# Loads of q, k and v moved to other slots of the pair loop, v split one slot earlier

## The chip, the cores and the metric

The kernel runs on one core of a Trainium2 chip. The metric is the time of one execution on the device, in microseconds. A core has five engines with queues of their own: TensorE (PE in the profile; its weight loads are PEld), VectorE (DVE), ScalarE (ACT), GpSimd (POOL) and SyncE (SP), which in this kernel issues all DMAs. Each engine works through its queue in order, and an instruction waits at the head of its queue until what it depends on is done.

## The reference

Sigmoid attention over 8 batches of 12 heads, 448 positions of 64 numbers, then a bilinear feed-forward network over all 3584 tokens:

```python
scores = scale * np.matmul(q, k.transpose(0, 1, 3, 2)) - np.log(S)
attn = 1.0 / (1.0 + np.exp(-scores))
x = np.matmul(attn, v)          # then heads side by side: 3584 x 768
a = x @ w1                      # 768 x 1024
b = x @ w2
h = a * b @ w3                  # 1024 x 1024
return h @ w_out                # 1024 x 768
```

The weights reach the kernel as 64-bit words, and are decoded to 32-bit numbers on the chip. Most products are made from a high and a low half of each operand, so that one product is three matmuls (hi x hi, hi x lo, lo x hi).

## The kernel before

The work is a loop over 48 **pairs** of heads (6 pairs to a batch, 8 batches), with four **slots** to a pair, one for each chunk of 128 keys (the last one has 64, and is taken second: `chunks` = 0, 3, 1, 2). Slot s belongs to pair s // 4. In a slot PE does the scores of its chunk (`scores` or, for the short chunk of a split pair, `short_scores`), then 12 matmuls of `up`, the feed-forward product of the batch before (`take(filler, ups)`, from slot 26 on; one output group `fc` takes three slots and ends with a store of `g`), then the product of the slot before with v (`attend_due`, tile `av`). `combine` makes x of a pair after its last attend: ScalarE and VectorE bring the two banks of `av` together in the tile `t`, and then split it into `xh`, `xl`.

Pairs 0 to 8 (`PLAIN` = 9) are **plain**: q and k are used as loaded, one tile `qp` for both. Pairs 9 to 47 are **split**: `split_pair` (lines 151 to 166) makes `qs` (two VectorE operations, lines 158 and 159), `kh` (VectorE, line 66), `kl` (POOL, line 67) and `ks` (four POOL copies, line 165), and needs the tiles `qq` and `kk`, one buffer each. `split_v` (168 to 176) makes `vs` by two VectorE casts and two POOL subtractions. All of `qp`, `qq` and `kk` share three buffers (tag `qk`); `vv` has two, the split tiles have two each.

`load_pair` (123 to 138) issues the loads of q and k, two DMAs for a plain pair and four for a split one; `load_v` (140 to 149) issues two or three. Before the change both are called at the start of a pair (lines 392 to 396): q and k for the pair after next, v for the next pair; v of the pair itself is split there too, and `split_pair` for the next pair is called in slot 1 (line 406).

Between these goes the decoding of the weights (`decode_weights`, 293 to 310), in 32 **jobs**: jobs 0 to 15 are w1 and w2, from 16 on w3. A job loads its words (`raw`, line 74), takes their magnitude on ScalarE (line 79), has six VectorE operations (lines 86 to 102), and is then split into halves (line 309, by lines 66 and 67). Jobs 0 to 11 have three buffers of words, loaded two jobs ahead; from job 12 on there is one buffer, and a job's words are loaded once the job before is decoded (line 303). Jobs 9 to 15 begin in slots 28, 29, 31, 32, 34, 35 and 38. Jobs 2 fc and 2 fc + 1 are first used by `up` in slot 26 + 3 fc of the passage.

The order of PE and SP is that of the program throughout (`manual_schedule`). That of ScalarE and POOL is, up to the start of pair 8; VectorE's order, and that of the other two from pair 8 on, is laid out by a planner ahead of the run, which goes by the place in the program and by when it thinks operands ready. Which of the free buffers of a tag a tile gets is also the planner's choice.

After the loop come the last batch's `up`, the product of w3 and w_out (line 484), and the final product with the stored `g` (line 500).

Of the kernel before, what the change touches and what calls it, by code (L numbers as in the profile page):

```python
# [25 lines left out]
def sigmoid_attention_bilinear_ffn(  # L26
# [22 lines left out]
    NC = len(CHUNKS)  # L49
# [6 lines left out]
    PLAIN = 9  # L56
# [8 lines left out]
    def split(dst_hi, dst_lo, src, hi_engine, lo_engine):  # L65
        hi_engine(out=dst_hi, in_=src)  # L66
        lo_engine.tensor_tensor(out=dst_lo, in0=src, in1=dst_hi, op=ALU.subtract)  # L67
# [55 lines left out]
    def load_pair(b, hp):  # L123
        heads = slice(2 * hp, 2 * hp + 2)
        if b * NPAIR + hp < PLAIN:

            qk = pa.tile([P, 2, S], F32, name="qp", tag="qk", bufs=3)
            for i, src in enumerate((qT, kT)):
                nc.sync.dma_start(out=qk[:, i], in_=src[b, heads].rearrange("h d s -> (h d) s"))
            return qk[:, 0], qk[:, 1]  # L130
        qq = pa.tile([P, 2, S], F32, name="qq", tag="qk", bufs=3)
        kk = pa.tile([P, 2, S], F32, name="kk", tag="qk", bufs=3)
        for dst, src in ((qq, qT), (kk, kT)):
            for r in range(2):
                nc.sync.dma_start(
                    out=dst[r * D:(r + 1) * D], in_=src[b, heads].rearrange("h d s -> d h s")
                )
        return qq, kk

    def load_v(b, hp):  # L140
        vv = pa.tile([P, NC, 2 * D], F32, name="vv")
        cols = slice(hp * 2 * D, (hp + 1) * 2 * D)
        full = (NC - 1) * P
        nc.sync.dma_start(
            out=vv[:, :NC - 1], in_=v[b, :full, cols].rearrange("(c p) e -> p c e", p=P)
        )
        for r in range(1 if b * NPAIR + hp < PLAIN else 2):
            nc.sync.dma_start(out=vv[r * D:(r + 1) * D, NC - 1], in_=v[b, full:, cols])
        return vv

    def split_pair(plain, qq, kk):

        if plain:
            return qq, kk, None, None
        qs = pf[0].tile([P, 2, S], F32R, name="qs")
        kh = pf[0].tile([P, 2, S], F32R, name="kh")
        kl = pf[0].tile([P, 2, S], F32R, name="kl")
        nc.vector.tensor_copy(out=qs, in_=qq)
        nc.vector.tensor_tensor(out=qs[D:], in0=qq[D:], in1=qs[D:], op=ALU.subtract)
        split(kh, kl, kk, nc.vector.tensor_copy, nc.gpsimd)  # L160

        ks = pf[0].tile([P, 2, P], F32R, name="ks")
        for j in range(2):
            for i, k in ((j, kh), (1 - j, kl)):
                nc.gpsimd.tensor_copy(out=ks[:, j, i * D:(i + 1) * D], in_=k[:, j, S - D:])
        return qs, kh, kl, ks

    def split_v(plain, vv):
        if plain:
            return vv  # L170

        vs = pf[0].tile([P, NC, 2, 2, D], F32R, name="vs")
        for j in range(2):
            split(vs[:, :, j, j, :], vs[:, :, j, 1 - j, :], vv[:, :, j * D:(j + 1) * D],
                  nc.vector.tensor_copy, nc.gpsimd)
        return vs
# [12 lines left out]
    def scores(qs, kh, kl, c):  # L189

        at, n = CHUNKS[c]
        sp = ps.tile([P, 2, 512], F32, name="sp", bufs=2)[:n, :, :S]
        for j in range(2):
            if kl is None:
                rows = slice(j * D, (j + 1) * D)
                nc.tensor.matmul(sp[:, j], kh[rows, at:at + n], qs[rows], start=True, stop=True)  # L196
                continue
            for m, k in enumerate((kh, kl)):
                nc.tensor.matmul(sp[:, j], k[:, j, at:at + n], qs[:, j], start=m == 0, stop=m == 1)  # L199
        return sp  # L200

    def attention(plain, sp):

        n = sp.shape[0]
        if plain:
            a = pa.tile([P, 2, S], F32, name="ap", tag="ah", bufs=3)[:n]
            sigmoid(a, sp)
            return (a,)
        ah = pa.tile([P, 2, S], F32R, name="ah", tag="ah", bufs=3)
        sigmoid(ah[:n], sp)  # L210
        sigmoid(sp, sp)
        if n < P:

            nc.vector.tensor_tensor(out=ah[n:], in0=sp, in1=ah[:n], op=ALU.subtract)
            return (ah,)
        al = pf[0].tile([P, 2, S], F32R, name="al")
        nc.vector.tensor_tensor(out=al, in0=sp, in1=ah, op=ALU.subtract)  # L217
        return ah, al

    def short_scores(ks, qs):  # L220


        sp = ps.tile([P, 2, 512], F32, name="sp", bufs=2)[:, :, :S]
        for j in range(2):
            nc.tensor.matmul(sp[:, j], ks[:, j], qs[:, j], start=True, stop=True)  # L225
        t = pf[0].tile([P, S], F32, name="st", bufs=1)
        add_halves(t, [sp[:, j] for j in range(2)])
        return t

    def short_attention(t):  # L230

        a = pa.tile([P, 2, S], F32R, name="ah", tag="ah", bufs=3)
        for j in range(2):
            rows = slice(j * D, (j + 1) * D)
            sigmoid(a[rows, j], t[rows])
        sigmoid(t, t)
        for j in range(2):
            rows, others = slice(j * D, (j + 1) * D), slice((1 - j) * D, (2 - j) * D)
            nc.vector.tensor_tensor(out=a[others, j], in0=t[rows], in1=a[rows, j], op=ALU.subtract)  # L239
        return (a,)  # L240
# [52 lines left out]
    def decode_weights():  # L293

        for i, (n, at, cs, _) in enumerate(jobs):
            if i + 2 < EARLY:
                load_job(i + 2)
            for k in (i, i + 1):
                if k not in fs and k in raws:
                    fs[k] = magnitude(raws[k])  # L300
            f = decode(raws.pop(i), fs.pop(i))
            if i + 1 >= EARLY and i + 1 < len(jobs):
                load_job(i + 1)
            if n == 3:
                nc.sync.dma_start(out=w3_dram[at, :, cs], in_=f)
                yield
                continue
            yield
            split(wh[n][:, at, cs], wl[n][:, at, cs], f, nc.scalar.copy, nc.vector)
            yield  # L310
# [24 lines left out]
    def take(stream, n):  # L335
        for _ in range(n):
            next(stream, None)
# [5 lines left out]
    pairs = [(b, hp) for b in range(B) for hp in range(NPAIR)]  # L343
# [8 lines left out]
    qks, vvs = {}, {}  # L352
    for p in range(2):
        qks[p] = load_pair(*pairs[p])
        load_job(p)
        if p == 0:
            vvs[0] = load_v(*pairs[0])
    splits, vs = {0: split_pair(0 < PLAIN, *qks.pop(0))}, {}
    weights = decode_weights()
    xs = {b: [] for b in range(B)}  # L360
    filler = iter(())
# [4 lines left out]
    def attend_due(slot):  # L366
        while waiting and waiting[0][0] <= slot:
# [6 lines left out]
            if c == NC - 2:  # L374
                b = pairs[p][0]
                xs[b].append(combine(b, accs.pop(p)))
                del vs[p]

    chunks = [0, NC - 1, *range(1, NC - 1)]
# [2 lines left out]
    for p, (b, hp) in enumerate(pairs):  # L384
        if p == PLAIN - 1:
            order.close()
            order.enter_context(tc.manual_schedule(engines={ET.PE, ET.SP}))
        plain = p < PLAIN
        if p == PLAIN - 1:
            phase_p.close()  # L390
            pf.append(phase_a.enter_context(tc.tile_pool(name="pf", bufs=2, side="right")))
        if p + 2 < len(pairs):
            qks[p + 2] = load_pair(*pairs[p + 2])
        if p + 1 < len(pairs):
            vvs[p + 1] = load_v(*pairs[p + 1])
        vs[p] = split_v(plain, vvs.pop(p))
        qs, kh, kl, ks = splits.pop(p)
        for i, c in enumerate(chunks):
            if not plain and i == 1:
                short = short_scores(ks, qs)  # L400
            else:
                sp = scores(qs, kh, kl, c)
                if not plain and i == 2:
                    waiting.append((slot + 1, p, NC - 1, short_attention(short)))
                waiting.append((slot + 1, p, c, attention(plain, sp)))
            if i == 1 and p + 1 < len(pairs):
                splits[p + 1] = split_pair(p + 1 < PLAIN, *qks.pop(p + 1))
            take(weights, steps.count(slot))
            if b > 0 and (hp, i) == (0, 2):
                take(filler, 10 ** 6)  # L410
                filler = up(b - 1, xs[b - 1], itertools.repeat("up"))
            take(filler, ups)
            attend_due(slot)
            slot += 1
# [124 lines left out]
```

## Time and profile before

| | |
|---|---|
| time, median of 3 runs | 1111.47 us (1111.01 to 1111.79) |
| the profiled execution | 1109.63 us, its span 1107.6 us |
| PE busy | 1070.8 us (97%), 5076 matmuls |
| DVE busy | 729.3 us (66%) |
| ACT busy | 563.0 us (51%) |
| POOL busy | 222.7 us (20%) |
| chain that ended last | PE 87%, DVE 6%, DMA 2%, ACT 2% |

Times in the rows are microseconds from the start of the span. A busy share is a mean over the whole span; matmuls are pipelined, so the duration of a single one (0.37 us) is longer than the distance from one to the next (0.2 us). An idle time in brackets stands before the instruction, with what ended it. A DMA row of SP is the issue, not the transfer.

### The profile page before, as it was taken

What the parts mean: (1) busy time and instruction counts of PE and PEld (TensorE: products, weight loads), DVE (VectorE), ACT (ScalarE), POOL (GpSimd) and SP (SyncE); (2) the same over time, 40 slices, a digit from 0 to 9 for tenths busy, and PEclk for the clock granted to TensorE, in tenths of its full rate; (3) what the DMA queues carried; (4) which work ended last, traced back from release to release, by engine and by line L of the source; (5) the groups of instructions that cost most, each with busy time, mean ns of one, the idle gap of its engine ahead of it and who ended that gap; (6) DMA issues with size and microseconds to landing.
All of it is one profiled execution on the core that took longest, in us unless ns stands there. A gap on an engine that the chain in (4) does not pass through costs nothing.

```text
span 1107.6 us, 14080 instructions
## 1 busy us (share of the span) xinstructions
PE 1070.8 (97%) x5076; PEld 910.5 (82%) x5076; DVE 729.3 (66%) x1073; ACT 563.0 (51%) x789; POOL 222.7 (20%) x277
## 2 busy tenths in 40 slices
PE   7996959999999999999999999999999999999998
PEld 1253749899899989989889999999999988888887
DVE  6876787788888878888797887857873132122221
ACT  5843647666776767767767776663342111011100
POOL 0001133243343333343333332400000000000000
PEclk9998979999999999999999999999999999999999
DMA  8634365444454434525454343206453021333211
GB/s 257 195 94 125 88 153 148 106 119 111 110 140 128 133 105 122 128 83 136 114 139 129 92 136 86 78 17 201 133 204 109 10 101 71 123 127 130 86 48 47
DMA packets 100692, 129.14 MB, mean 117 GB/s; under 512 B 8016, under 2 KB 82960, under 8 KB 100624
## 3 DMA queue, kind: packets, MB, share of 16 engines
q1 hardware_dynamic: 100624, 128.25, 39.7%
q8 instruction: 40, 0.66, 0.2%
q14 instruction: 28, 0.23, 0.1%
HBM read 98.34 MB, written 29.88 MB: 116 GB/s over the span
## 4 chain that ended last, share of the span: by engine, by line
PE 87%; DVE 6%; DMA 2%; ACT 2%; issue 1%; SPq 1%; POOL 0%; DVEq 0%; POOLq 0%; ACTq 0%
PE up L320 39%; PE up L500 21%; PE av L255 10%; PE sp L199 8%; PE up L484 6%; DMA raw<-w 2%; PE sp L225 1%; PE sp L196 1%; PE av L248 1%; DVE raw L99 1%; DVE f L94 1%; ACT f L79 1%; DVE raw L86 1%; DMA vv<-vL 1%; DVE al L217 1%
## 5 line engine op out<-in xcount | busy, mean ns | idle before, releaser
L320 PE MATMUL up<-xh,w 128*128 128x448 f32 x1536 | 468.2, 368 | 2.3 <-DVE g L331 2.3
L320 PEld LDWEIGHTS up<-xh,w 128*128 128x128 f32 x1536 | 288.9, 188 | 35.7 <-issue 5.3
L320 PE MATMUL up<-xl,w 128*128 128x448 f32 x768 | 281.6, 367 | 0.0
L500 PE MATMUL up<-w 128*128 128x512 f32 x1008 | 228.7, 389 | 0.0
L500 PEld LDWEIGHTS up<-w 128*128 128x128 f32 x1008 | 189.2, 188 | 39.3
L180 ACT ACTIVATE ah<-sp,bias 128x896 fp32r<-128x896 f32 x117 | 117.8, 1006 | 97.2 <-PE sp L199 97.1
L217 DVE TENSOR_TENSOR al<-sp,ah 128x896 fp32r<-128x896 f32 x117 | 127.5, 1090 | 44.2 <-ACT sp L180 42.5
L320 PEld LDWEIGHTS up<-xl,w 128*128 128x128 f32 x768 | 144.5, 188 | 12.9
L67 POOL TENSOR_TENSOR kl<-kk,kh 128x896 fp32r<-128x896 f32 x39 | 104.5, 2678 | 246.4 <-DVE kh L66 195.0
L510 DVE COPY o_sb<-up 128x512 f32<-128x512 f32 x42 | 29.0, 691 | 161.0 <-PE up L500 161.0
L66 ACT CAST w<-graw 128x1024 fp32r<-128x1024 f32 x28 | 29.3, 1055 | 174.7 <-PE up L500 170.5
L67 POOL TENSOR_TENSOR vs<-vv,vs 128x256 fp32r<-128x256 f32 x78 | 67.2, 874 | 251.8 <-DVE vs L66 182.7
L255 PE MATMUL av<-ah,vs 128*128 128x448 f32 x312 | 103.7, 373 | 13.9 <-POOL vs L67 12.7
L180 ACT ACTIVATE sp<-sp,bias 128x896 f32<-128x896 f32 x117 | 113.8, 973 | 0.0
L199 PE MATMUL sp<-qs,kh 128*128 128x448 f32 x234 | 86.3, 369 | 0.0
L199 PE MATMUL sp<-qs,kl 128*128 128x448 f32 x234 | 86.2, 368 | 0.0
L255 PE MATMUL av<-al,vs 128*128 128x448 f32 x234 | 86.2, 368 | 0.0
L239 DVE TENSOR_TENSOR ah<-st,ah 64x448 fp32r<-64x448 f32 x78 | 56.1, 719 | 40.0 <-ACT st L180 38.8
L255 PEld LDWEIGHTS av<-ah,vs 128*128 128x128 f32 x312 | 58.7, 188 | 25.4 <-POOL vs L67 13.7
L79 ACT ACTIVATE f<-raw 128x768 f32<-128x768 f32 (+2 forms) x48 | 34.1, 711 | 64.5 <-DMA raw<-w 28.2
L86 DVE TENSOR_SCALAR raw<-raw 128x768 uint32<-128x768 uint32 (+2 forms) x48 | 35.6, 743 | 38.1 <-ACT f L79 37.9
L186 ACT COPY t<-av 64x448 f32<-64x448 f32 x78 | 41.2, 529 | 34.0 <-PE av L255 33.0
(54 smaller groups left out, 1289.3 us busy)
## 6 DMA issues: line engine op xcount, KB each, us to landing
qq<-qT SPq DMA_DIRECT2D x78, 224.0 KB, 3.6
kk<-kT SPq DMA_DIRECT2D x78, 224.0 KB, 3.8
g_dram<-g SPq DMA_DIRECT2D x64, 224.0 KB, 1.9
graw<-g_dram SPq DMA_DIRECT2D x14, 1024.0 KB, 5.3
raw<-w SPq DMA_DIRECT2D x16, 768.0 KB, 6.2
out<-o_sb SPq DMA_DIRECT2D x42, 256.0 KB, 2.0
vv<-vL SPq DMA_DIRECT2D x48, 192.0 KB, 3.8
raw<-w3T SPq DMA_DIRECT2D x16, 512.0 KB, 4.9
```

The lines of the kernel that those rows point to most:

```text
L67: lo_engine.tensor_tensor(out=dst_lo, in0=src, in1=dst_hi, op=ALU.subtract)
L79: nc.scalar.activation(f, raw[..., 1].bitcast(F32), AF.Abs, scale=HW_SCALE)
L86: nc.vector.tensor_scalar(out=high, in0=high, scalar1=0x80000000, scalar2=0x80000000, op0=ALU.bitwise_and, op1=ALU.bitwise_xor,)
L180: nc.scalar.activation(dst, src, AF.Sigmoid, bias=bias[:n], scale=scale)
L186: nc.scalar.copy(out=dst[rows], in_=src[j][others])
L199: nc.tensor.matmul(sp[:, j], k[:, j, at:at + n], qs[:, j], start=m == 0, stop=m == 1)
L217: nc.vector.tensor_tensor(out=al, in0=sp, in1=ah, op=ALU.subtract)
L239: nc.vector.tensor_tensor(out=a[others, j], in0=t[rows], in1=a[rows, j], op=ALU.subtract)
L255: nc.tensor.matmul(accs[j][:, :S], v[:, c, j].rearrange("p u d -> p (u d)"), a[:, j], start=first and m == 0, stop=last and m == len(ops) - 1,
L320: nc.tensor.matmul(acc[:, :S], w[:, fc, kc], x, start=(kc == 0 and m == 0), stop=(kc == NK - 1 and m == 2),)
L484: nc.tensor.matmul(acc[:, :NM], a[:, jc], w[:, jc, ms], start=(jc == 0 and m == 0), stop=(jc == NF - 1 and m == 2),)
L500: nc.tensor.matmul(acc[:, :TB], w[:, fc, ms], g[:, at, fc % NH], start=(fc == 0 and m == 0), stop=(fc == NF - 1 and m == 2),)
```

## The change

`load_pair`, `load_v` and the two splits are called from a new function, `prepare(p, i)`, ahead of the scores in slot i of pair p. For the next pair n = p + 1: `split_pair` in slot 1 (in slot 2 for pairs 9 and 10); `load_v` in slot 0 for plain pairs and in slot 1 for split ones; `split_v` in slot 3. For the pair after next, n = p + 2: `load_pair` in slot 0 for plain pairs and in slot 2 for split ones, except for pairs 9 and 10, which are loaded in slot 0 of the pair right before them (pair 9 in slot 32, pair 10 in slot 36). Where both a load of v and one of q and k fall into one slot, v now goes first.

```diff
-    splits, vs = {0: split_pair(0 < PLAIN, *qks.pop(0))}, {}
+    splits, vs = {0: split_pair(0 < PLAIN, *qks.pop(0))}, {0: split_v(0 < PLAIN, vvs.pop(0))}
...
+    def prepare(p, i):
+
+        n = p + 1
+        change = n in (PLAIN, PLAIN + 1)
+        if i == (2 if change else 1) and n < len(pairs):
+            splits[n] = split_pair(n < PLAIN, *qks.pop(n))
+        if i == 0 and change:
+            qks[n] = load_pair(*pairs[n])
+        if i == (0 if n < PLAIN else 1) and n < len(pairs):
+            vvs[n] = load_v(*pairs[n])
+        if i == NC - 1 and n < len(pairs):
+            vs[n] = split_v(n < PLAIN, vvs.pop(n))
+        n = p + 2
+        if i == (0 if n < PLAIN else 2) and n not in (PLAIN, PLAIN + 1) and n < len(pairs):
+            qks[n] = load_pair(*pairs[n])
...
-        if p + 2 < len(pairs):
-            qks[p + 2] = load_pair(*pairs[p + 2])
-        if p + 1 < len(pairs):
-            vvs[p + 1] = load_v(*pairs[p + 1])
-        vs[p] = split_v(plain, vvs.pop(p))
         qs, kh, kl, ks = splits.pop(p)
         for i, c in enumerate(chunks):
+            prepare(p, i)
...
-            if i == 1 and p + 1 < len(pairs):
-                splits[p + 1] = split_pair(p + 1 < PLAIN, *qks.pop(p + 1))
```

## Rows read from the trace of the kernel before

**Rows 1.** The page: PE's busy tenths in 40 slices of the span.
```profile
PE   7996959999999999999999999999999999999998
```
**Rows 2.** PE's waits: line, waited for, us in total, times, longest us.
```profile
PE av L255 <- POOL vs L67: 12.7, 1, 12.7
PE av L248 <- ACT ap L180: 10.8, 3, 9.1
...
PE av L255 <- DVE t L187: 0.6, 2, 0.5
```
**Rows 3.** Busy time by stretches: PE, PEld, DVE, ACT, POOL (instructions), PEclk, DMA share, GB/s.
```profile
80.00:100.00 20.00, 10.92 (x40) 6.07 (x40) 7.28 (x12) 6.60 (x8) 0.00 (x0) 0.74 0.46 137
...
140.00:160.00 20.00, 7.27 (x28) 5.82 (x27) 17.47 (x25) 7.19 (x11) 6.62 (x7) 0.66 0.72 170
...
160.00:744.00 584.00, 582.84 (x2835) 530.49 (x2834) 475.45 (x693) 410.38 (x585) 206.59 (x254) 1.00 0.42 112
```
**Rows 4.** PE in order of time, 76 to 125 us: start, us, instruction, idle before.
```profile
80.84 1.02 PE L196 MATMUL sp<-qp 64*128 64x448 f32 x4
...
93.61 1.76 PE L248 MATMUL av<-ap,vv 128*64 128x448 f32 x4 [9.08 <-ACT ap L180]
95.30 1.87 PE L196 MATMUL sp<-qp 64*128 64x448 f32 x4
...
101.32 0.97 PE L196 MATMUL sp<-qp 64*64 64x448 f32 x4
...
114.81 0.47 PE L199 MATMUL sp<-qs,kh 128*128 128x448 f32 x1
```
**Rows 5.** SP in order of time, 62 to 85 us.
```profile
81.91 1.25 SPq L135 DMA_DIRECT2D kk<-kT  x2
...
84.44 0.52 SPq L74 DMA_DIRECT2D raw<-w  x1
```
**Rows 6.** ACT in order of time, 76 to 160 us.
```profile
91.77 0.89 ACT L79 ACTIVATE f<-raw 128x768 f32<-128x768 f32 x1 [17.15 <-DMA raw<-w]
```
**Rows 7.** PE in order of time, 125 to 162 us.
```profile
130.80 0.47 PE L320 MATMUL up<-xh,w 128*128 128x448 f32 x1 [2.33 <-DVE g L331]
...
133.37 0.37 PE L199 MATMUL sp<-qs,kh 128*128 128x448 f32 x1
...
137.46 0.57 PE L225 MATMUL sp<-qs,ks 128*128 128x448 f32 x2
...
153.22 0.74 PE L255 MATMUL av<-ah,vs 128*128 128x448 f32 x1 [12.73 <-POOL vs L67]
...
155.21 0.57 PE L199 MATMUL sp<-qs,kh 128*128 128x448 f32 x1
```
**Rows 8.** SP in order of time, 72 to 156 us.
```profile
108.41 1.25 SPq L135 DMA_DIRECT2D kk<-kT  x2
...
111.53 13.15 SPq L74 DMA_DIRECT2D raw<-w  x2
...
136.16 0.37 SPq L74 DMA_DIRECT2D raw<-w  x1
...
137.97 1.25 SPq L135 DMA_DIRECT2D kk<-kT  x2
...
148.92 0.37 SPq L74 DMA_DIRECT2D raw<-w3T  x1
```
**Rows 9.** DVE in order of time, 76 to 160 us.
```profile
104.64 0.96 DVE L102 TENSOR_TENSOR f<-f,raw 128x768 f32<-128x768 f32 x1
...
106.50 2.70 DVE L67 TENSOR_TENSOR w<-f,w 128x768 fp32r<-128x768 f32 x1 [0.36 <-ACT w L66]
...
148.81 0.62 DVE L66 CAST kh<-kk 128x896 fp32r<-128x896 f32 x1
```
**Rows 10.** POOL in order of time, 100 to 160 us.
```profile
149.56 2.20 POOL L67 TENSOR_TENSOR kl<-kk,kh 128x896 fp32r<-128x896 f32 x1 [31.43 <-DVE kh L66]
```
**Rows 11.** ACT's waits in 0 to 60 us: waited for, us in total, times, longest us.
```profile
ACT f L79 <- DMA raw<-w: 3.3, 1, 3.3
```

## The prediction

> **What bounds the kernel now.** I read the page's slices first [rows 1]: PE is at nine tenths almost everywhere, with three dents, in slices 1, 4 and 6 (each 27.7 us wide). The list of PE's waits names what is behind the later two [rows 2]: 12.7 us for one POOL subtraction of `split_v`, 10.8 us in three waits for a plain sigmoid, the longest 9.1. Busy time by stretches places them [rows 3]: 80 to 100 us and 140 to 160 us are half empty, at a mean granted clock of 0.74 and 0.66, while from 160 to 744 us PE is busy 582.84 of 584 us. So nothing before PE matters in 37 of the 48 pairs, and the whole question is what happens between 80 and 157 us, at the passage from plain to split pairs. I name PE's places by slots (four to a pair, slot 36 is the first of pair 9), counted from the first `up` matmul, which the code puts into slot 26.
>
> First stop. Slot 31 begins its scores at 80.84, slot 32 at 95.30, slot 33 at 101.32, slot 36 at 114.81 [rows 4]; an undisturbed slot is (114.81 - 101.32) / 3 = 4.50. So slot 31 lost 9.96 and slot 32 another 1.52; the matmuls behind the 9.08 of idle time ran at the lower clock level (four of them took 1.76 and 1.87 where 1.02 is usual). Sum 11.48. Its chain: the sigmoid that PE wants stands in ScalarE's queue behind the magnitude of weight job 11, which waited 17.15 us for its words [rows 6]; these were issued at 84.44, because SP stood until 81.91 at the second tile of pair 9, whose buffer is pair 7's and comes free with the last scores of slot 31 [rows 5]. A load that nobody needed for 30 us held up one that was due.
>
> Second stop: 2.33 us in slot 39, an `up` bank waiting for `g` [rows 7].
>
> Third stop: slot 41 begins at 137.46, slot 42 at 155.21; of these 17.75 us 12.73 were idle, and the four attends behind it took 1.99 at the lower clock instead of 0.8 (2835 matmuls in 584 us are 0.206 each) [rows 3, 7]. Lost: 13.9, and some 0.6 more in slot 42. The whole passage loses 11.5 + 2.3 + 13.9 + 0.6 = 28.3 us. Behind the third stop SP shows a chain: raw words have one buffer from job 12 on, so each load waits until the job before is decoded, and everything behind it on SP waits too. Job 13's words went out at 111.53 (after pair 10's keys had waited for POOL until 108.41), job 14's just before 124.68, job 15's at 136.16, the next at 148.92 [rows 8]: 12.3 us a job, then 12.8. Pair 11 and the v of pair 10 stand behind job 15's words (137.97), their casts come at 148.81, POOL's work at 149.56 [rows 8 to 10], and PE had them at 153.22.
>
> **The change part by part.** No instruction is added or taken away; 2 to 4 loads of q and k, 2 or 3 of v, 3 VectorE and 5 POOL operations of a pair's split and 2 and 2 of v's change their places.
>
> *Plain pairs, v issued ahead of q and k.* Same instructions in the same slot; a pair's words may leave later by the two q and k issues, which I put at 0.8 us. In 0 to 60 us ScalarE waited for words once, 3.3 us [rows 11], and that was a load of the prologue, which does not move. I take 0; if the words did decide, 7 pairs x 0.8 = 5.6 us is the upper end. A gain I exclude: PE's waits in this stretch are not for v or q past the first loads, but for sigmoids [rows 2].
>
> *Pair 9 loaded in slot 32 instead of 28.* SP reaches the v of pair 8 in slot 28, whose attend ends about 71.8 (slot 29 begins two slots before 80.84). Job 11's words then go out at 71.8 + 1.3 = 73.1 and, with the 7.33 us from issue to the magnitude's start (84.44 to 91.77) [rows 5, 6], that magnitude runs at 80.4, the sigmoid behind it is done by 82.4, and PE asks at 93.61 - 9.08 = 84.53. Margin 2.1 us: the first stop goes whole, 11.5 us. What hides it is that margin; if the words landed 4 us later, 2 of the 11.5 stay. Pair 9 now lands around 93, its split takes some 5 us on VectorE and POOL, and slot 36 asks at 80.84 + 5 x 4.5 = 103.35. Covered by about 5 us.
>
> *Pair 10 loaded in slot 36, split in slot 38, v in slots 37 and 39.* Here is the price. On SP this load now stands behind the words of jobs 13, 14 and 15, with one buffer among them. I walk it: VectorE needed from 92.66 (end of job 11's magnitude) to 105.60 for jobs 11 and 12 [rows 6, 9], 12.94 us, of which I estimate 1.6 to be the first split's operations that now come later. From a magnitude done at 81.3 that gives 92.6 for job 13's words (94.2 if nothing comes off). Two more jobs at 11.5 to 12.8 each, 12.0 taken (12.8 is the slowest pace [rows 8]; 11.5 is an estimate: half of 12.94 - 1.6, the 0.9 of a magnitude [rows 6], and for the landing the 4.9 that 12.3 leaves beside half of 12.94 and 0.9): job 15's words at 116.6 (115.6 to 119.8). From there to POOL's end on the pair loaded right behind them the trace has one case, 136.16 to 151.76 [rows 8, 10], 15.6 us, in which VectorE wove job 15's decode between; with the split ahead of that decode, as its place in the program now allows, I estimate 11. VectorE's order is fixed by the planner and the trace of before cannot show the new one; I take 13. So pair 10 is ready at 129.6 (126.6 to 135.4).
> PE, undisturbed, would begin slot 40 at 103.35 + (133.37 - 114.81 - 2.33) = 119.6 [rows 4, 7]. A new wait of 10.0 us (7.0 to 15.8) for `kh`/`kl` of pair 10, and after a wait of this length the trace shows the lower clock both times: 1.5 to 2.1 us more, I take 2. Together 12. The second stop lies inside this wait and adds nothing. The v of pair 10 lands with k and is split while slot 40 runs: off the path.
>
> *Later pairs.* q and k two slots later, v one, split of v one slot earlier, all through SP, VectorE and POOL. The loads have a pair's time of reserve, and PE has 1.2 us of idle in 584 to give [rows 3]: a gain of at most that, and what is left of the 0.6 us of waits for `t` [rows 2]. Cost 0, with the rival below as the other end.
>
> Sum: 28.3 - 12.0 = 16.3 us, in the profiled execution's time 1109.63 - 16.3 = 1093.3; the median of the runs lies 1.84 above that execution, so 1111.47 - 16.3 = 1095.2. Bounds of the new wait: 28.3 - 8.5 = 19.8 and 28.3 - 17.9 = 10.4, that is 1091.7 to 1101.1.
>
> **The rivals.**
> *A, forecast:* the wait at slot 40, 1091 to 1101.
> *B, the chain is shorter than I think.* With PE not stopped, VectorE works in other company, and if the planner puts split and loads well, slot 40 waits under 3 us and, as after the 2.33 us of rows 7, the clock stays up. Gain 25 to 28: 1084 to 1086, with the stretch up to 1091 between. Against it: the single buffer makes the three loads follow one another whatever the order.
> *C, a second wait.* The planner sets the casts of pair 10 in VectorE's queue ahead of `al` and `g` of pair 9, which then stand behind a DMA; PE stops before slot 40 and the held work of two or three operations follows. One blocked job is 5.7 us: 1095.2 + 6 = about 1101 to 1107.
> *D, slower.* The split of the next pair moves, in VectorE's order, from the end of a pair to slots 0 and 1, where the two additions into `t` free the banks that the next attend needs. PE waited there up to 0.5 us [rows 2]. If each of the 37 pairs from 11 on paid 0.5, that is 18.5: 1095.2 + 18.5 = 1113.7. It decides from 16.3 / 37 = 0.44 us a pair. What speaks for it: a VectorE subtraction that met POOL's `kl` took 2.70 where the operation of the same shape before it took 0.96 [rows 9], 1.7 longer. The Trainium skill says why (SBUF - State Buffer, section "SBUF: two separate sides"): VectorE and GpSimd share one port pair under an exclusive lock, and a VectorE operation with two SBUF inputs stands until a GpSimd operation that reads SBUF is through. The row agrees; by this rule the additions into `t`, with one input in PSUM, are not held, only what stands before them. Against D: before, the same number of splits ran in these pairs, and PE lost 1.2 us.
> *E, it does not do what it says:* job 11's words still come late, for another reason on SP, and the new wait eats the rest: about 1111.
>
> **How the numbers follow.** A 0.57, B with the stretch beside it 0.18, C 0.10, D 0.09, E 0.06. The predicted time is A's, 1095.2. The range takes A whole, B's to 1084 and C's up to 1104: 1084 to 1104. About 0.2% (2.2 us) is what a measurement of this kernel can tell from no change: faster by more 0.85 (A, B, C), within it 0.06 (E), slower 0.09 (D).
>
> **What would show it.** Right: no load of pair 9 on SP before slot 31's scores end; PE without a gap at 84 us; one new wait of 7 to 16 us on scores (not attends), near 119 us, put down to a DMA, VectorE or POOL of pair 10, with the words of job 15 leaving SP just before pair 10's q; from then on no wait over 0.6 us. Wrong: no such wait (B), waits before attends or `up` (C), `t` as releaser in most pairs (D), the gap at 84 us still there (E). The forecast falls with the pace of jobs 13 to 15: each microsecond a job moves it by two.

## The result and the profile after

The changed kernel takes 1099.95 us in the median of 4 runs (1098.64 to 1102.10), the kernel before beside it 1111.63. The ratio is 0.9896, 95% interval 0.9876 to 0.9915. In a later comparison (the run after_again below) it was 0.9867 (0.9844 to 0.9889). So it is 1.0 to 1.3% faster. The prediction, 1095.2, is 0.9854 of its 1111.47: inside the second interval and below the first. The time is in the range, and the wait that was forecast is there, but it is 4.2 us long and not 10; other losses and one gain that were not forecast stand beside it, and in part they cancel.

The page of the kernel after, PE's busy tenths and clock, against [rows 1] (slices counted from 1): the dent of slice 4 is gone, that of slice 6 is at 8 tenths, and slice 5 has a new one, at 6.
```profile
PE   7999689999999999999999999999999999999998
...
PEclk9999899999999999999999999999999999999999
```
PE's waits of the kernel after, columns as in [rows 2]: the two long ones are gone, and many short ones have come.
```profile
PE av L248 <- ACT ap L180: 4.2, 2, 3.7
...
PE sp L199 <- DVE kh L66: 2.4, 1, 2.4
PE av L255 <- DVE al L217: 2.1, 1, 2.1
PE sp L199 <- POOL kl L67: 1.9, 1, 1.9
PE up L320 <- DVE g L331: 1.8, 1, 1.8
PE sp L199 <- DVE st L187: 1.7, 1, 1.7
```
Busy time by stretches of the kernel after, columns as in [rows 3]. The passage is full up to 100 us. From 160 to 744 us PE's busy time rises by 0.45 us only, but PE issues 2851 matmuls where it issued 2835.
```profile
80.00:100.00 20.00, 20.00 (x91) 11.86 (x90) 17.92 (x25) 7.88 (x11) 2.11 (x1) 1.00 0.35 103
140.00:160.00 20.00, 16.93 (x76) 14.61 (x75) 18.63 (x26) 10.71 (x16) 6.19 (x8) 0.94 0.36 108
160.00:744.00 584.00, 583.29 (x2851) 534.64 (x2850) 463.85 (x692) 411.42 (x586) 177.96 (x252) 1.00 0.42 113
```
For all kernels I compare four stretches, each the distance between the first score matmuls of two slots on PE's timeline, in us. Before slot 8 a profiled execution may be some us late with its first loads (slot 8 starts at 22.6 to 26.5), which says nothing of a kernel, and from slot 191 to the end before and after take the same 368.8 us.

| kernel | slots 8 to 31 | 31 to 36 | 36 to 48 | 48 to 191 | ratio to before |
|---|---|---|---|---|---|
| before | 57.64 | 33.97 | 64.34 | 559.64 | 1 |
| after | 61.76 | 22.52 | 66.91 | 556.31 | 0.9896 |
| after_again | 61.72 | 22.52 | 64.02 | 555.78 | 0.9867 |
| e1_plain_order_back | 57.67 | 22.51 | 63.94 | 555.22 | 0.9824 |
| e2_only_9_and_10 | 57.65 | 22.52 | 68.33 | 559.66 | 0.9923 |
| e4_pair10_ahead_of_words | 61.59 | 22.52 | 60.80 | 554.70 | 0.9842 |
| e5_only_9 | 56.92 | 22.51 | 59.98 | 561.60 | 0.9855 |
| e6_both_mends | 57.26 | 22.52 | 60.58 | 555.14 | 0.9803 |
| e8_pair10_early | 57.23 | 22.52 | 62.15 | 555.19 | 0.9839 |
| e7_words_in_halves | 57.67 | 22.52 | 57.36 | 554.67 | 0.9774 |
| e9_split_v_back | 57.63 | 22.51 | 61.14 | 554.70 | 0.9813 |
| e10_split_pair_back | 57.65 | 22.52 | 56.93 | 556.49 | 0.9780 |
| e11_loads_back | 57.28 | 22.52 | 62.63 | 560.81 | 0.9851 |

The intervals of the ratios reach 0.002 to 0.003 to either side. Where an expectation speaks of slots 31 to 48, it is the sum of two columns; where it names the start of slot 31, the first column tells the same. Each row is one profiled execution. The first three rows hold the whole result: from 8 to 31 after loses 4.1, from 31 to 36 it gains 11.45, from 36 to 48 it loses 2.6 (in after_again it gains 0.3), from 48 to 191 it gains 3.3 (3.9). In the last stretch the three kernels with the later pairs as before (before, e2, e5) take 559.6 to 561.6, and all with q and k of the later pairs in slot 2 take 554.7 to 556.5.

**The loss ahead of slot 31.** SP of the kernel after, in order of time, 10 to 30 us (start, us, instruction):
```profile
17.31 0.38 SPq L144 DMA_DIRECT2D vv<-vL  x1
...
18.27 0.58 SPq L129 DMA_DIRECT2D qp<-qT  x1
...
19.43 1.08 SPq L74 DMA_DIRECT2D raw<-w  x2
```
The load of v waits for its buffer, which comes free with an attend of the pair before, and q and k now wait behind it. They go out at 18.27, and the weight words right behind them. In the run e1, where q and k are ahead again, they go at 14.92, the first v at 17.68 and the words at 18.70. The busy share of the DMA engines is 0.15 in 15 to 17 us and 0.20 in 17 to 19 (0.81 and 0.31 in e1): they stood idle first and had everything at once then. ACT of the kernel after, with the idle time and its cause in brackets:
```profile
27.40 0.89 ACT L79 ACTIVATE f<-raw 128x768 f32<-128x768 f32 x1 [4.40 <-DMA raw<-w]
```
And PE of the same kernel behind it:
```profile
29.23 1.48 PE L248 MATMUL av<-ap,vv 128*64 128x448 f32 x4 [3.70 <-ACT ap L180]
30.64 1.86 PE L196 MATMUL sp<-qp 64*128 64x448 f32 x4
```
The words left only 0.7 us later than in e1, as the prediction reckoned, but took 7.9 us to land instead of 5.1: the magnitude starts at 27.40 where e1 has it at 25.01 with no wait for words. The sigmoid that PE wants stands behind it, and the matmuls behind PE's idle 3.70 took 1.48 and 1.86 where 1.02 is usual; the granted clock of 29 to 33 us is 0.57.

**The passage.** SP of the kernel after, 60 to 130 us:
```profile
67.53 1.31 SPq L135 DMA_DIRECT2D qq<-qT  x2
...
85.53 1.27 SPq L135 DMA_DIRECT2D kk<-kT  x2
...
98.65 0.37 SPq L74 DMA_DIRECT2D raw<-w  x1
...
110.55 0.37 SPq L74 DMA_DIRECT2D raw<-w  x1
...
122.65 0.37 SPq L74 DMA_DIRECT2D raw<-w  x1
123.07 1.30 SPq L135 DMA_DIRECT2D qq<-qT  x2
```
Pair 9's keys leave after slot 31's scores (84.46), as before [rows 5], but the words of job 11 (76.63) are now ahead of them, so they hold nothing up. Pair 9's q still goes out at 67.53, ahead of the v of pair 8 (75.61), though the code now calls this load in slot 32: in this place SP's order is not that of the program, and no run shows why. It costs nothing here, as SP waits for the buffer of v until 75.59 in any case. Jobs 13, 14 and 15 follow 11.9 and 12.1 us apart, and pair 10 stands behind the third. PE of the kernel after, 105 to 160 us:
```profile
111.11 0.47 PE L320 MATMUL up<-xh,w 128*128 128x448 f32 x1 [1.82 <-DVE g L331]
...
120.41 0.47 PE L255 MATMUL av<-al,vs 128*128 128x448 f32 x1 [2.07 <-DVE al L217]
121.90 0.71 PE L255 MATMUL av<-ah,vs 128*128 128x448 f32 x1 [1.02 <-DVE xl L67]
...
134.15 0.44 PE L199 MATMUL sp<-qs,kh 128*128 128x448 f32 x1 [2.36 <-DVE kh L66]
...
136.46 0.74 PE L199 MATMUL sp<-qs,kl 128*128 128x448 f32 x1 [1.88 <-POOL kl L67]
...
151.90 0.44 PE L199 MATMUL sp<-qs,kh 128*128 128x448 f32 x1 [1.73 <-DVE st L187]
```
The forecast wait on the scores of slot 40 is there, for `kh` and `kl`, but it is 4.2 us and not 10. Before it PE already lost time, at `g` (with the clock at 0.57 behind it, 111 to 115 us), `al` and `xl`, and after it at `st`. What `al` and `xl` stand behind shows on ACT of this kernel, the magnitude of job 14:
```profile
115.82 0.89 ACT L79 ACTIVATE f<-raw 128x768 f32<-128x768 f32 x1 [3.53 <-DMA raw<-w]
```
The sigmoid of slot 36, which `al` of pair 9 needs, comes after it, at 116.62, though its scores were done at 108.06; the cast `xh` of pair 8, which `xl` needs, comes at 118.82.

### The profile page after: what moved, and what is told of

The parts are those of the page before. It is cut to its first block, busy times and chain, and to the rows that moved or that the text cites. A ratio compares the mean times of both kernels' runs of the same rounds, so it can differ in the third digit from the quotient of the medians.

```text
span 1099.0 us, 14114 instructions
## 1 busy us (share of the span) xinstructions
PE 1072.5 (98%) x5076; PEld 913.8 (83%) x5076; DVE 717.4 (65%) x1073; ACT 564.0 (51%) x789; POOL 196.8 (18%) x277
## 4 chain that ended last, share of the span: by engine, by line
PE 85%; DVE 6%; DMA 4%; ACT 2%; issue 2%; SPq 1%; POOL 0%; DVEq 0%; ACTq 0%
PE up L320 38%; PE up L510 21%; PE av L255 10%; PE sp L199 8%; PE up L494 6%; DMA raw<-w 3%; PE sp L225 1%; DVE f L94 1%; ACT f L79 1%; DVE raw L99 1%; DVE f L102 1%; PE av L248 1%; DVE w L67 1%; PE sp L196 1%; DVE raw L86 0%
## 5 line engine op out<-in xcount | busy, mean ns | idle before, releaser
L67 POOL TENSOR_TENSOR kl<-kk,kh 128x896 fp32r<-128x896 f32 x39 | 88.5, 2268 | 417.9 <-DVE kh L66 401.9
L67 POOL TENSOR_TENSOR vs<-vv,vs 128x256 fp32r<-128x256 f32 x78 | 70.9, 919 | 99.5 <-DVE vs L66 82.4
L180 ACT ACTIVATE ah<-st,bias 64x448 fp32r<-64x448 f32 x78 | 52.2, 669 | 4.0 <-DVE st L187 2.1
```

The costliest lines, as they stand in the source:

```text
L180: nc.scalar.activation(dst, src, AF.Sigmoid, bias=bias[:n], scale=scale)
```

## The experiments

### The order of v, q and k in the plain pairs

Theory: the 4 us ahead of slot 31 come from v standing ahead of q and k, and nothing else. Edit to the changed kernel:
```diff
+        if i == 0 and p + 2 < PLAIN:
+            qks[p + 2] = load_pair(*pairs[p + 2])
         n = p + 1
...
-        if i == (0 if n < PLAIN else 2) and n not in (PLAIN, PLAIN + 1) and n < len(pairs):
+        if i == 2 and n > PLAIN + 1 and n < len(pairs):
```


> The changed kernel, but in plain pairs q and k are issued ahead of v again, as before. Theory (plain order): in the changed kernel a sigmoid of slot 8 stood 4.40 us behind the magnitude of a weight job whose words had not landed, PE stood 3.70 us at 29.2 us and ran some 1.2 us at the lower clock behind it; the cause is v's place ahead of q and k. Then this kernel has no PE wait over 1.1 us between 20 and 60 us, slot 31 begins near 80.9 instead of 84.5, and the time falls by 3 to 5 us, to 1095 to 1097. Rival (the wait is a matter of when the words are issued in any order, or of chance in the transfers): the 3.7 us wait stays or comes and goes, slot 31 begins at 83 or later, and the time stays within 1.5 us of 1099.95. A second rival: the lead of 3.6 us is taken back at slot 40, if the words of jobs 13 to 15 set that slot and do not move; then slot 31 is early, but slot 44 is not, and the time does not change.


Measured: 1093.24 us (1091.57 to 1095.81), ratio 0.9824 (0.9803 to 0.9844). Slots 8 to 31 take 57.67 again, as before the change. So the swap (v ahead of q and k) costs 4.1 us in this stretch. Behind it the words of job 13 leave 11.6 us after slot 31 begins (14.2 in after, 12.5 in after_again), and slots 36 to 48 take 63.94: 3 us less than in after, but the same as in after_again. So a further loss down the chain of jobs is not shown. PE of this kernel at slot 40:
```profile
127.36 0.44 PE L199 MATMUL sp<-qs,kh 128*128 128x448 f32 x1 [2.28 <-DVE kh L66]
129.67 0.74 PE L199 MATMUL sp<-qs,kl 128*128 128x448 f32 x1 [1.87 <-POOL kl L67]
```
Without the swap's loss, PE goes on with pair 10's `kl` at 129.67; the prediction had pair 10 ready at 129.6.

### Pair 9 alone, and pairs 9 and 10 alone

Edits to the kernel before. First, only pair 9 is loaded in slot 32 and split in slot 34, with pair 10's load right behind it:
```diff
-        if p + 2 < len(pairs):
+        if p + 1 == PLAIN:
+            qks[p + 1] = load_pair(*pairs[p + 1])
+        if p + 2 < len(pairs) and p + 2 != PLAIN:
             qks[p + 2] = load_pair(*pairs[p + 2])
...
+            if i == 2 and p + 1 == PLAIN:
+                splits[p + 1] = split_pair(p + 1 < PLAIN, *qks.pop(p + 1))
...
-            if i == 1 and p + 1 < len(pairs):
+            if i == 1 and p + 1 < len(pairs) and p + 1 != PLAIN:
```


> The kernel before, with pair 9 alone moved (loaded in slot 32, split in slot 34); pair 10 is loaded right behind it in slot 32, as before, and so SP stands there until pair 9's split has freed its buffers. Theory (the first stop is pair 9's load alone; what comes after is set by the chain of the words of jobs 13 to 15): the 9.1 us wait at 84 us and the slower matmuls behind it go, 11.5 us; the words of job 13 leave only behind pair 10, near 100 to 103 us against 111.5 before, and those of job 15 near 125 to 128 against 136.2; the third stop, for v of pair 10 behind them, stays at 12 to 16 us in slot 41. Time 1099 to 1103, so hardly other than with pair 10 moved too (e2). Rival (pair 10's late load is what the gain needs): the words of job 13 leave as late as before, the third stop grows by what the first gave, and the time is within 3 us of the kernel before.


Measured: 1097.75 (1094.88 to 1098.48), ratio 0.9855 (0.9836 to 0.9875). Slots 31 to 36 take 22.51: moving pair 9 alone (its load, and its split behind it) takes the whole first stop away. The expectation for the rest missed. The third stop, 12.73 us in [rows 7], did not stay; with the words no longer late it shrank to this, on PE:
```profile
138.67 0.47 PE L255 MATMUL av<-ah,vs 128*128 128x448 f32 x1 [3.53 <-POOL vs L67]
```
So most of the third stop was a consequence of the first, and this one move is about as good as the whole change.

Second, pairs 9 and 10 are both moved as in the change, the rest stays:
```diff
-        if p + 2 < len(pairs):
+        if p + 2 < len(pairs) and p + 2 not in (PLAIN, PLAIN + 1):
             qks[p + 2] = load_pair(*pairs[p + 2])
+        if p + 1 in (PLAIN, PLAIN + 1):
+            qks[p + 1] = load_pair(*pairs[p + 1])
...
+            if i == 2 and p + 1 in (PLAIN, PLAIN + 1):
+                splits[p + 1] = split_pair(p + 1 < PLAIN, *qks.pop(p + 1))
...
-            if i == 1 and p + 1 < len(pairs):
+            if i == 1 and p + 1 < len(pairs) and p + 1 not in (PLAIN, PLAIN + 1):
```


> The kernel before, with pairs 9 and 10 alone moved (loaded in slot 0 of the pair right before them, split in slot 2); plain pairs, later pairs and the splits of v stay as they were. Theory: the gain is these two pairs, 28.3 us of waits at the passage against some 20 new ones, so 8 to 13 us faster than before: 1099 to 1104; the first stop at 84 us is gone, and waits at slots 36 to 44 stand in its place. The moves of the later pairs were worth the 3 us by which the changed kernel ran faster from slot 48 on; they are missing here, so from slot 48 to slot 191 this kernel takes as long as the one before (559.6 us). Rival (the v moves matter at the passage, as v of pair 10 is now split in slot 39): without them v of pair 10 comes late in slot 41 as before, PE waits there for POOL's subtraction of vs for over 5 us, and the gain is under 5 us.


Measured: 1104.99 (1102.22 to 1106.94), ratio 0.9923 (0.9906 to 0.9940). This edit isn't the isolation I meant: in slot 36 it puts pair 11's loads ahead of pair 10's, and SP then stood from 119.56 to 131.31 inside pair 10. SP of this kernel:
```profile
119.56 1.25 SPq L135 DMA_DIRECT2D qq<-qT  x2
131.31 1.25 SPq L135 DMA_DIRECT2D kk<-kT  x2
```
PE of this kernel at slot 40:
```profile
136.44 0.71 PE L199 MATMUL sp<-qs,kh 128*128 128x448 f32 x1 [14.70 <-DVE kh L66]
```
It settles two other things. Slots 48 to 191 take 559.66, as in before, so the moves of the later pairs, which it leaves out, are worth the 3.3 to 3.9 us there. And PE came to slot 40 at 136.44 - 14.70 = 121.74 with 1.4 us of waits ahead of it since slot 36: the price of one late load of q and k is here up to 14.7 us, by where SP comes to it.

### Pair 10 out from behind the words

Edit to the changed kernel: q, k and v of pair 10 are issued in slot 35, ahead of job 15's words.
```diff
-        if i == 0 and change:
+        if i == 0 and n == PLAIN:
             qks[n] = load_pair(*pairs[n])
-        if i == (0 if n < PLAIN else 1) and n < len(pairs):
+        if i == (0 if n < PLAIN else 1) and n < len(pairs) and n != PLAIN + 1:
...
+        if i == NC - 1 and n == PLAIN:
+            qks[n + 1] = load_pair(*pairs[n + 1])
+            vvs[n + 1] = load_v(*pairs[n + 1])
```


> The changed kernel, but pair 10's q, k and v are issued in slot 35, ahead of the words of job 15, instead of in slots 36 and 37 behind them. Theory (the words' single buffer holds pair 10): pair 10 leaves SP near 111 to 116 us instead of 123 to 128, its kl is done before 127 instead of at 136.4, the waits of slot 40 for kh and kl (2.4 and 1.9 us, with the slower matmuls behind them 7 to 9 us in all) go, and the time falls by 5 to 9 us, to 1091 to 1095. The waits of slots 36 to 38 (g, al, xl: 4.9 us of idle) stay, as they come from the magnitude of job 14 that waits for its words. Rival (VectorE is what is full at the passage, not the queue of loads): kl of pair 10 is still done after 133 us, or as much waiting turns up at other operations of VectorE in slots 40 to 44, and the time stays within 2 us of 1099.95.


Measured: 1096.00 (1093.37 to 1097.62), ratio 0.9842 (0.9822 to 0.9862). Pair 10's keys leave at 110.06, ahead of job 15's words (119.94), and PE waits for neither `kh` nor `kl`. Slots 36 to 48 shrink to 60.80; 3 to 6 us were lost behind those words.

The same edit together with that of e1:


> The changed kernel with two edits at once: q and k of the plain pairs issued ahead of v again, and pair 10's q, k and v issued in slot 35, ahead of job 15's words. Theory (two separate losses: SP standing at v's buffer in the first 30 us, and pair 10 standing behind the single buffer of words): the gains add. Slot 31 at 80.8, no wait for kh or kl at slot 40, slots 31 to 48 in 79 to 84 us, time 1087 to 1090 where before is 1111.5, ratio 0.978 to 0.981. Rival (the passage has one bound, VectorE's decode of jobs 13 to 15, so that what is gained ahead of it is lost in it): 1092 to 1094, ratio 0.983 or more, with the waits at slot 40 or at al in slots 37 to 39 longer than in either edit alone.


Measured: 1089.62 (1089.06 to 1092.32), ratio 0.9803 (0.9780 to 0.9827). The two losses are separate and their mends add: 57.26 and 60.58 in the table.

Then from e1 on, pair 10's q and k in slot 32, right behind pair 9's, and nothing else moved:
```diff
-        if i == 0 and change:
+        if i == 0 and n == PLAIN:
             qks[n] = load_pair(*pairs[n])
+            qks[n + 1] = load_pair(*pairs[n + 1])
```


> The kernel with q and k of the plain pairs ahead of v again, and pair 10's q and k issued in slot 32 right behind pair 9's, and nothing else moved: only pair 10's load differs from the run e1_plain_order_back. Theory (moving pair 10's load to slot 36 is itself a loss, since it then stands behind three loads of words with one buffer): the waits for kh and kl at slot 40 go (2.3 and 1.9 us with 1 to 2 us of slower matmuls behind), slots 31 to 48 in 80 to 83 us instead of 86.45, time 1087 to 1090. Rival (a load in slot 32 holds SP at its buffer until pair 8's scores are read, and so delays the words of jobs 12 and 13 by 4 to 7 us): slots 31 to 48 in 86 us or more, time 1093 or more, with ScalarE's magnitude of job 12 or 13 waiting over 4 us.


Measured: 1094.05 (1090.95 to 1094.93), ratio 0.9839 (0.9813 to 0.9866), the same as e1 within the intervals. Slots 36 to 48 take 62.15, between the theory's and the rival's. The waits for `kh` and `kl` are gone, but SP stood at pair 10's buffers until 96.96, and job 13's words went out at 98.30, 15.1 us behind the start of slot 31 (11.6 in e1). ACT of this kernel, job 13's magnitude:
```profile
104.90 0.93 ACT L79 ACTIVATE f<-raw 128x768 f32<-128x768 f32 x1 [6.04 <-DMA raw<-w]
```
PE of this kernel, the two longest waits that are left:
```profile
119.82 0.71 PE L255 MATMUL av<-ah,vs 128*128 128x448 f32 x1 [3.54 <-DVE xl L67]
...
145.17 0.53 PE L199 MATMUL sp<-qs,kh 128*128 128x448 f32 x1 [3.06 <-DVE st L187]
```
So a load too early costs the words, a load too late costs the scores, and slot 35 is between.

### The words of jobs 12 to 15 in halves

Edit to e6: the one buffer becomes two of half the size, and each of these jobs is loaded and decoded in two halves.
```diff
-            raw = pd.tile([P, NK, P, 2], U32, name="raw", bufs=1)[:, :src.shape[1]]
+            raw = pd.tile([P, NF // 2, P, 2], U32, name="raw", bufs=2)[:, :src.shape[1]]
...
+            raws[i] = [load_words(src[:, h:h + NK // 2]) for h in (0, NK // 2)]
```


> The kernel with both mends (e6_both_mends), and the words of jobs 12 to 15 loaded as two halves into two half buffers, so that the first half of the next job's words can be under way while the second half of a job is decoded; the arithmetic is the same in twice as many operations of half the size for these four jobs. Theory (the waits for al and xl in slots 37 and 38 arise because ScalarE stands at a magnitude whose words have one buffer): ScalarE's waits for words in 100 to 130 us fall from 3 us or more a job to under 1, the waits for al and xl go or halve, slots 31 to 48 become 2 to 4 us shorter, 0.2 to 0.4% of the whole. Rival (VectorE's own work, some 10 us a job, sets the pace of jobs 13 to 15): waits for words fall but al and xl stay late, and the time is the same within 1 us or longer by the more numerous operations.


Measured: 1086.22 (1085.60 to 1086.94), ratio 0.9774 (0.9750 to 0.9798), 0.3% below e6; slots 36 to 48 take 57.36 instead of 60.58. ACT's waits for words in 90 to 160 us (line, waited for, us in total, times, longest) were these in e6:
```profile
ACT f L79 <- DMA raw<-w: 5.9, 2, 3.6
```
and are these in this kernel:
```profile
ACT f L313 <- DMA raw<-w: 2.9, 3, 1.7
```
They halve, but don't fall under 1 us each, and at `al` and `xl` PE still waits 1.80 and 0.69 (2.21 and 1.02 in e6). What went is mostly at slots 42 and 43, 9.32 us instead of 12.95, where PE of e6 waited 2.29 for `st`. So the single buffer is part of these waits and not the whole of them, and most of the 3.2 us came from elsewhere: in this kernel VectorE has the second addition into `st` ahead of the casts of v, as in e10 below. The median is the lowest of all versions; that of e10 (0.9780) lies within its interval.

### Which move of the later pairs is worth 3 to 4 us

Three edits to e6, one move of pairs 11 to 47 put back in each. The split of v in slot 0 of its own pair:
```diff
-        if i == NC - 1 and n < len(pairs):
+        if i == NC - 1 and n <= PLAIN + 1:
             vs[n] = split_v(n < PLAIN, vvs.pop(n))
+        if i == 0 and p > PLAIN + 1:
+            vs[p] = split_v(False, vvs.pop(p))
```


> The kernel with both mends (e6_both_mends), with the split of v for pairs 11 to 47 put back into the first slot of its own pair. Theory (the 3 to 5 us that slots 48 to 191 gained come from the casts of v, which no longer stand ahead of the additions into t in the first slot of a pair): slots 48 to 191 take 558 to 560 us as before the change instead of 554.7 to 556.3, time 3 to 5 us above e6_both_mends. Rival (they come from q, k and v landing elsewhere, or from the order of the split of q and k): within 1 us of e6_both_mends, slots 48 to 191 in 555 to 556.


Measured: 1090.51 (1089.34 to 1091.98), ratio 0.9813 (0.9788 to 0.9838); slots 48 to 191 in 554.70. The theory fell: the split of v changes nothing here.

The split of q and k behind the scores of slot 1:
```diff
-        if i == (2 if change else 1) and n < len(pairs):
+        if i == (2 if change else 1) and n <= PLAIN + 1:
...
+            if i == 1 and PLAIN + 1 < p + 1 < len(pairs):
+                splits[p + 1] = split_pair(False, *qks.pop(p + 1))
```


> The kernel with both mends (e6_both_mends), with the split of q and k for pairs 11 to 47 put back behind the scores of slot 1, where it stood before the change. Theory (the 3 to 5 us that slots 48 to 191 gained come from q and k being loaded in slot 2, so that SP no longer stands at a buffer that the split of the next pair still reads): within 1 us of e6_both_mends, slots 48 to 191 in 554.5 to 556. Rival (they come from the split standing ahead of the scores, and so earlier in VectorE's and POOL's order): slots 48 to 191 in 558 to 560, time 3 to 5 us longer.


Measured: 1088.07 (1087.66 to 1089.16), ratio 0.9780 (0.9761 to 0.9800). Slots 48 to 191 take 556.49, 1.35 more than e6 and not the rival's 3 to 5. What moved is the passage, 56.93 instead of 60.58. The reason is in VectorE's order. Slot 43's scores need the bank that two additions into `st` bring free. DVE of e6 in slots 41 and 42:
```profile
137.10 1.08 DVE L159 TENSOR_TENSOR qs<-qq,qs 64x896 fp32r<-64x896 f32 x1
...
139.40 0.62 DVE L187 TENSOR_TENSOR st<-sp,st 64x448 f32<-64x448 f32 x1
139.94 2.12 DVE L66 CAST vs<-vv 128x256 fp32r<-128x256 f32 x2
...
142.77 0.63 DVE L187 TENSOR_TENSOR st<-sp,st 64x448 f32<-64x448 f32 x1
```
Both additions stand behind VectorE's part of pair 11's split, and the second also behind two casts of v, which took 2.12 while POOL was at `kl` (139.50 to 141.68). PE waited 2.29 for it. In e10 both stand ahead of these casts, which take 0.49 there, the first also ahead of `qs`, and PE has no wait for `st`. DVE of e10:
```profile
134.87 0.62 DVE L187 TENSOR_TENSOR st<-sp,st 64x448 f32<-64x448 f32 x1
135.52 1.09 DVE L159 TENSOR_TENSOR qs<-qq,qs 64x896 fp32r<-64x896 f32 x1
...
137.29 0.63 DVE L187 TENSOR_TENSOR st<-sp,st 64x448 f32<-64x448 f32 x1
```
In the changed kernel itself it was `qs` that held them, beside `kl` from 146.00 to 148.38:
```profile
146.43 2.90 DVE L159 TENSOR_TENSOR qs<-qq,qs 64x896 fp32r<-64x896 f32 x1
149.36 0.62 DVE L187 TENSOR_TENSOR st<-sp,st 64x448 f32<-64x448 f32 x1
```

The loads of q and k in slot 0 instead of slot 2:
```diff
-        if i == 2 and n > PLAIN + 1 and n < len(pairs):
+        if i == 0 and n > PLAIN + 2 and n < len(pairs) or i == 2 and n == PLAIN + 2:
             qks[n] = load_pair(*pairs[n])
```


> The kernel with both mends (e6_both_mends), with the loads of q and k for pairs 12 to 47 put back from slot 2 to slot 0. Theory (the 3 to 5 us of slots 48 to 191 come from these loads: in slot 0 SP stands at the buffers of the pair that is split in slot 1, and the words of w3 and the stores of g behind it go out later): SP's waits for the splits' POOL operations come back (82 us in 23 waits in 180 to 720 us before the change), slots 48 to 191 in 558 to 560, time 3 to 5 us above e6_both_mends. Rival (the order of the splits does it, and the loads have a pair's time of reserve): within 1 us of e6_both_mends, slots 48 to 191 in 554.5 to 556.


Measured: 1095.80 (1095.29 to 1098.10), ratio 0.9851 (0.9830 to 0.9872), 0.5% above e6; slots 48 to 191 take 560.81. So it is the loads. SP's waits in 180 to 720 us in e11, columns as above:
```profile
SPq L135 <- POOL kl L67: 47.6, 15, 5.4
SPq L135 <- POOL ks L165: 43.4, 11, 6.7
```
The same two in e6:
```profile
SPq L135 <- POOL ks L165: 1.0, 5, 0.2
SPq L135 <- POOL kl L67: 0.7, 1, 0.7
```
Issued in slot 0, the loads stand at buffers that the split in slot 1 still reads. In slot 2 they don't.

How PE loses the 5.7 us shows in the starts of its matmuls, not in its list of waits, which has 1.5 us for `t` in e11. The usual distance from one start to the next is 0.204 us. In slots 48 to 191 of e11, 35 matmuls start later than that, by 6.1 us in all; in e6 there are two, with 0.45 us. Of the 35, 31 are in the first attends of a pair, which need the banks that the additions into `t` bring free. Each of those stands in a slot in which VectorE ends the decode of a w3 job. All 15 such decodes of this stretch end in slot 1 of a pair in e11; in e6 they end earlier, in slot 3 of the pair before or in the first 3.8 us of slot 0. DVE of e11, the end of a decode and the two additions, where slot 76 begins at 276.39:
```profile
281.25 0.69 DVE L102 TENSOR_TENSOR f<-f,raw 128x512 f32<-128x512 f32 x1
...
283.39 1.27 DVE L187 TENSOR_TENSOR t<-av,t 64x448 f32<-64x448 f32 x2
```
PE of e11 behind it:
```profile
284.15 0.44 PE L255 MATMUL av<-ah,vs 128*128 128x448 f32 x1 [0.64 <-DVE t L187]
```
And DVE of e6, where slot 76 begins at 274.98:
```profile
272.95 0.68 DVE L102 TENSOR_TENSOR f<-f,raw 128x512 f32<-128x512 f32 x1
...
279.44 1.27 DVE L187 TENSOR_TENSOR t<-av,t 64x448 f32<-64x448 f32 x2
```
So the decode of w3 is the link: in e11 it stands right ahead of `t`, and in e6 it doesn't. The theory had its words leave SP later; that holds for 9 of the 14 words issued in this stretch. How much is the words' landing and how much the planner's order was not separated.

### The changed kernel once more

> The changed kernel once more, beside the two runs of this call. Theory: ratio 0.988 to 0.991 to the kernel before, slot 31 at 84.5, slots 31 to 48 in 89.4 us and slots 48 to 191 in 556.3, as in its first profile, since these come from the order of the queues. Rival (the single profile was a chance one): any of these off by over 1 us, and the losses named from it are not to be trusted.


Measured: 1097.73 (1096.03 to 1100.40), ratio 0.9867 (0.9844 to 0.9889). Three of the four stretches repeat within 0.6 us. Slots 36 to 48 are 2.9 shorter: the wait for `g` in slot 36 and the low clock behind it (3.3 us of slot 36) are absent, with job 13's words 1.5 us earlier. So the expectation missed in slots 36 to 48, and a loss there holds only as far as both profiles show it. That wait was the chance of one profile; those for `al`, `kh`, `kl` and `st` are in both.

## Why the prediction was right and where it was wrong

**The first stop went whole.** Forecast 11.48, measured 11.45 (slots 31 to 36), and e5 shows that pair 9's load alone does it. The margin of 2.1 us held: PE and job 11's words both came some 3.5 us later than reckoned, by the loss ahead of slot 31. Of the signs that were set for this, the gap at 84 us is gone, but "no load of pair 9 on SP before slot 31's scores end" is true of its keys and not of its q (67.53).

**The new wait has the mechanism forecast, but not the size.** Pair 10 stood behind job 15's words; their pace was 11.9 and 12.1 (forecast 12.0), from there to the end of `kl` it took 136.41 - 122.65 = 13.76 (forecast 13), and without the plain swap's loss the time itself, 129.67, is the forecast's. e4 and e6, which take it out from behind the words, gain what was left of it. The wait is 4.2 us where 7.0 to 15.8 was forecast, since PE came to it late.

**The plain swap was mis-sized:** taken as 0 with an upper end of 5.6, it measured 4.1. The step that failed is "a pair's words may leave later by the two q and k issues". I looked at what the words lose in issue time, 0.8, and it was 0.7. I did not ask what the load of v itself waits for: it waits for a buffer, holds q and k behind it, and then all of them go out at once with the words, which took 2.8 us longer to land.

**"PE, undisturbed, would begin slot 40" at 119.6 and "from then on no wait over 0.6 us" failed.** In e1, where slot 36 begins at 103.26 as forecast, PE asks for slot 40 at 127.36 - 2.28 = 125.08. It lost time before, at `al` of pair 9 and `xl` of pair 8, which stand in the queues of ScalarE and VectorE behind a magnitude or a decode that waits for words. That is rival C's kind of wait, beside A's and not instead of it, though what stands ahead is job 14's decode and not pair 10's casts. In part these waits only shift the same loss forward, as slot 40's wait shrank to 4.2. Together with the wait at `st` (1.73, with `qs` lengthened to 2.90, both in the kernel after) slots 36 to 48 came out 2.6 us longer than before (0.3 shorter in after_again), where 16.8 of removed stops and 12 of new wait had promised 4.8 less. The lengthening is the one that rival D named, but at one place and for `st`, not for `t` in each pair. The Trainium skill (SBUF - State Buffer, section "SBUF: two separate sides") has VectorE and GpSimd share a port pair under an exclusive lock; the trace agrees: `qs` ended at 149.33, `kl` at 148.38, and `qs` takes 1.09 by itself.

**The later pairs gained 3.3 to 3.9, not 0.** The step that failed is "PE has 1.2 us of idle in 584 to give". A single matmul shows 0.37 us, and the next one starts 0.2 after it; a gap of up to 0.16 between them is covered and counts as busy. The counts of [rows 3] and of the same stretch after, 2835 and 2851, held what the idle time hid: 16 matmuls by 0.206 are 3.3 us. The starts show where: in slots 48 to 191 of before, 33 matmuls start late, by 4.9 us in all, every one in the first attends of a pair, which need the banks that `t` brings free; in the kernel after they are 8, with 1.7 us. This is the place that rival D named. The kernel before already lost there, and the change took most of it away instead of adding to it.

The errors: +4.1 for the swap, +4.5 to +7.4 in slots 36 to 48, -3.3 to -3.9 later. They cancel in part, and that the time came so near the forecast is to that extent luck: the medians gained 11.7 and 15.3 us against 16.3, the profiled executions 8.7 and 12.1 (the one of before lies 1.8 to 2 us under its median).

## What to carry to other kernels

Before a load is moved ahead of others on a queue, look up what it waits for: a load that waits for its buffer holds back everything behind it, and the best place is the slot in which the buffer is just free, neither earlier (e8, e11) nor behind a load with one buffer (the change itself). When a stall is removed, ask which of the later stalls were only its echo (e5), and spread a forecast wait over all queues that hang on the same late data. Read whether an engine has time to give from the number of its instructions in a stretch and from the distance of their starts, not from its idle time.

## What the runs showed of the hardware

Two orders of the same loads in the same slot had the words land 3.5 us later (27.31 instead of 23.77 us), with an issue only 0.7 us later. A `kl` subtraction of one shape took 2.22 us in the mean in e6 and 2.73 in e11, over 34 pairs each, and the VectorE operation that it starts beside goes with it: the 22 of e11 that start inside the subtraction `qs` took 2.96 to 2.99, while 24 of e6 that start beside none, or beside `al`, took 2.11 to 2.13. And the length of a short wait doesn't tell the granted clock behind it: in the kernel after it was 0.57 of the upper level, near the lower one, in 111 to 115 us, behind 1.82 us of idle at `g`, and 1.00 in 152 to 156 us, behind 1.73 at `st`, as it was 1.00 in 131 to 135 us of before, behind the 2.33 of [rows 7]. The prediction's "the clock stays up" after a wait under 3 us is therefore not a rule.
